# Evicting attention scores and v from PSUM: one strided read over four banks, contiguous writes, two engines

## The chip, the cores and the metric

The kernel runs on one core of a Trainium2 chip. The metric is the device time of one execution in microseconds (us), lower is better. Every kernel is therefore compared by its ratio to the kernel before in the same call.

Engine names: PE is TensorE (matmuls), PEld its weight loads, DVE is VectorE, ACT is ScalarE, POOL is GpSimd, SP the queue that issues the DMAs. PEclk is the share of TensorE's clock that was granted. PSUM is the memory that matmuls write to; this kernel uses it as 8 banks of 512 fp32 in each of 128 partitions. To evict is to copy a result from PSUM to SBUF, the engines' working memory; the profile calls these copies CAST. "L280" is line 280 of the kernel that is being shown. Lines differ by a few between kernels; the text says which is which.

## The reference, cut to what matters

```python
def _A_ref(x, wqkv, wo):            # S = 2048, D = 1024, 32 heads of 32
    q, k, v = ...                   # (x @ wqkv), split in heads
    idx = pos[:, None] - off[None, :]          # 8 keys per position, every second one
    logits = einsum('bhsd,bhswd->bhsw', q, k[idx]) * scale
    o = einsum('bhsw,bhswd->bhsd', softmax(masked logits), v[idx])
    return o @ wo
def _B_ref(x, w_in, w_sp, b_sp, w_out):        # gated MLP
    z = gelu(x @ w_in); z1, z2 = z[..., :Fh], layernorm(z[..., Fh:])
    return (z1 * (w_sp @ z2 + b_sp)) @ w_out
g = sigmoid((x * gate_w).sum(-1)); return g * A + (1 - g) * B
```

## The kernel before

The order of the work is: z2 (first quarter), attention in 8 groups of 4 heads, the rest of z2, z1, then the spatial and output stages. The change touches attention.

TensorE computes scores of 128 queries against a band of 135 keys. A *band set* is one to three such tiles for the 4 heads of a group. Head `h` goes to bank `4 + h`. ScalarE casts them to f16 in a staging tile where the 4 heads lie side by side, and a DMA writes them to DRAM, from where they come back sheared (shifted by one key from query to query) so that VectorE can work on 8 keys a query.

```python
def v_tile(hf, j):
    ps = low_bank()                                # banks 0 to 3
    ...  # 8 matmuls, 512 columns                                            (L250)
    nc.scalar.copy(_sub_ap(st, (j % 4) * 512, [[C, 4], [1, HG], [HG, DH]]),  # (L253)
                   ps[:].rearrange("p (g h d) -> p g h d", g=4, h=HG))
    ...  # DMA to v_d after every fourth tile

def band_set(g, x):                                # x = 0 .. 5
    ...
    for m in range(n):                             # n = 2, 3, 3, 3, 3, 2
        for h in range(HG):                        # HG = 4, KW = 135
            nc.tensor.matmul(banks[4 + h][:, m * KW + lo:(m + 1) * KW], ...)   # (L275)
    for h in range(HG):
        src = banks[4 + h][:, 0:n * KW].rearrange("p (m k) -> p m k", m=n)[:, :, lo:KW]
        nc.scalar.copy(st[:, 0:n, lo:KW, h], src)                             # (L280)
    ...  # DMA to band_d

for g in range(NG):                                # 8 groups
    main = ...   # q/k tiles of the next group (L243, cast in L245); v tiles in groups 0 and 3
    for x in range(6):
        band_set(g, x)
        ...      # a sixth of main after each set
    attend(g)    # VectorE: softmax, attn * v (L315 to L319); ScalarE: exp (L300)
...
for f in range(NF):                                # z1: 14 blocks
    for c in range(4):
        ...                                        # 8 matmuls (L425)
        nc.scalar.activation(z1s[:, c, :], ps[:], ACT.Gelu_apprx_tanh)       # (L427)
    sync.dma_start(z1_d[...], z1s)                 # z1s: one of two slots
...
load_raw(1)   # 8 transposing DMAs of half of w_sp (L183); the scheduler moves them up
```

An element of the band cast goes to `st[..., h]`, 4 f16 elements from the last: an 8-byte stride. The v cast also writes with an 8-byte stride.

## Time and profile before

Median 784.95 us (784.42 to 785.49, 2 runs).

| stretch (us) | what | what limits it |
|---|---|---|
| 66 to 327 | attention | ScalarE busy 228 of 261 us |
| 327 to 380.6 | rest of z2 | TensorE |
| 380.6 to 478.6 | z1 | TensorE |
| 478.6 to 786 | spatial, output | TensorE |

The table of stretches of the kernel before. Columns: busy us and number of instructions of PE, PEld, DVE, ACT, POOL, then granted TensorE clock, DMA share, GB/s.

```profile
core 0: us, PE busy (x) PEld busy (x) DVE busy (x) ACT busy (x) POOL busy (x), PEclk, DMA share, GB/s
66.00:327.00 261.00, 209.86 (x1235) 96.08 (x1235) 136.66 (x131) 228.21 (x307) 0.00 (x0) 0.90 0.52 145
```

The list by line, shapes kept apart, of the kernel before: count, then busy us and mean ns of one, then idle time before it. L280 is one of the four band casts, L253 the v cast, L245 the q/k cast, L493 a VectorE instruction that reads 512 fp32 from PSUM.

```profile
L280 ACT CAST arena<-bank_73 128x405 f16<-128x405 f32 x32 | 37.9, 1186 | 0.0
L253 ACT CAST arena<-bank_69 128x512 bf16<-128x512 f32 x8 | 11.6, 1450 | 0.0
L245 ACT CAST arena<-bank_67 128x512 bf16<-128x512 f32 x16 | 9.6, 598 | 13.2 <-PE bank_67 L243 13.2
L493 DVE TENSOR_TENSOR arena<-bank_69,arena 128x512 f16<-128x512 f32 x7 | 4.8, 686 | 0.7 <-PE bank_69 L435 0.6
```

The q/k cast reads with an 8-byte stride and writes contiguously: 598 ns for 512 elements. The v cast reads contiguously and writes with a stride: 1450 ns for as many. The band cast takes 1186 ns for 405.

The timeline of ScalarE in the kernel before (start, duration):

```profile
273.67 1.17 ACT L280 CAST arena<-bank_72 128x405 f16<-128x405 f32 x1
274.57 1.17 ACT L280 CAST arena<-bank_73 128x405 f16<-128x405 f32 x1
275.47 1.17 ACT L280 CAST arena<-bank_74 128x405 f16<-128x405 f32 x1
```

Neighbours overlap, so the rate is in the starts: 0.90 us apart, 2.2 ns an element.

The list of waits of the kernel before, 66 to 327 us (us in total, times, longest):

```profile
PE bank_74 L275 <- ACT arena L280: 13.5, 23, 0.7
PE bank_73 L275 <- ACT arena L280: 11.5, 21, 0.7
PE bank_71 L275 <- ACT arena L280: 10.3, 4, 4.9
PE bank_72 L275 <- ACT arena L280: 4.5, 10, 0.7
```

TensorE waits 39.8 us for ScalarE to free the band banks.

The chain of waits around the start of z1 (start, us, what), kernel before:

```profile
391.00 1.74 PE bank_69 L425 x8
392.74 0.07 SPq L183
...
405.06 3.57 DMA z_d<-arena
...
408.74 0.61 ACT arena L427
...
409.39 1.89 PE bank_71 L425 x8
```

```profile
406.37 1.89 PE L425 MATMUL bank_70<-arena 128*128 128x512 bf16 x8
409.39 1.89 PE L425 MATMUL bank_71<-arena 128*128 128x512 bf16 x8 [1.12 <-ACT arena L427]
```

The chain runs through transposes (L183) at 392.7 to 405, then a z1 write, then the cast that needed the slot.

### The profile page before, as it was taken

To read this page: it belongs to the slowest core of one execution; us is meant where nothing else is said; L and a number is where in the kernel's file an instruction comes from. 1 tells how busy PE (TensorE), PEld (TensorE's weight loads), DVE (VectorE), ACT (ScalarE), POOL (GpSimd) and SP (SyncE) were. 2 spreads that over 40 slices of the span, in tenths; PEclk is the share of its full clock that TensorE was granted. 3 is DMA by queue.
4 is the path that set the end of the run, shared out by engine and by line. 5 is a ranking of instruction groups with operands and counts; after the bars stand their busy time and mean duration, and the time that the engine had idled before them with its cause. 6 is when DMAs were issued, how large, how long until landed. Compare 5 with 4: busy or idle time off the path is not lost.

```text
span 785.7 us, 9516 instructions
## 1 busy us (share of the span) xinstructions
PE 720.4 (92%) x3672; PEld 335.9 (43%) x3672; DVE 361.6 (46%) x462; ACT 402.9 (51%) x649; POOL 6.0 (1%) x13
## 2 busy tenths in 40 slices
PE   5997868799778887899999999999999999999998
PEld 3554423355333333455444444444444444444443
DVE  1000027487192756795120008667888478332310
ACT  3456968999699889998523332212211121222221
POOL 0000000000000000001000000000000000000000
PEclk9999887999989779999999999999999999999999
DMA  8998563565426335605996242433646459983111
GB/s 213 243 98 127 157 178 117 157 179 139 120 85 195 106 125 164 197 2 142 214 220 179 76 133 81 108 77 84 213 109 168 121 114 205 183 163 95 52 41 40
DMA packets 238716, 106.45 MB, mean 135 GB/s; under 512 B 182864, under 2 KB 232016, under 8 KB 238672
## 3 DMA queue, kind: packets, MB, share of 16 engines
q1 hardware_dynamic: 237632, 105.86, 54.2%
q8 instruction: 28, 0.46, 0.3%
q10 hardware_dynamic: 1040, 0.00, 0.1%
q14 instruction: 16, 0.13, 0.0%
HBM read 45.10 MB, written 45.00 MB: 115 GB/s over the span
## 4 chain that ended last, share of the span: by engine, by line
PE 55%; SPq 2%; ACT 1%; DMA 1%; DVE 0%; issue 0%; ACTq 0%; DVEq 0%
PE bank_72 L435 6%; PE bank_71 L435 5%; PE bank_67 L435 5%; PE bank_68 L435 5%; PE bank_74 L435 5%; PE bank_70 L435 5%; PE bank_73 L435 3%; PE bank_69 L435 3%; SPq L183 2%; PE bank_71 L425 1%; PE bank_69 L425 1%; PE bank_67 L425 1%; PE bank_72 L425 1%; PE bank_68 L425 1%; PE bank_73 L425 1%; PE bank_74 L425 1%
## 5 line engine op out<-in xcount | busy, mean ns | idle before, releaser
L435 PEld LDWEIGHTS <-arena 128*128 128x128 f16 (+1 forms) x1400 | 137.0, 98 | 166.5 <-issue 1.6
L243 PEld LDWEIGHTS <-arena 128*128 128x128 bf16 x512 | 50.9, 104 | 67.7 <-issue 20.2
L210 PEld LDWEIGHTS <-arena 128*128 128x128 bf16 x512 | 50.3, 99 | 49.8 <-issue 5.0
L315 DVE TENSOR_TENSOR arena<-arena,att_A 128x8192 f16<-128x8192 bf16 x16 | 70.7, 4421 | 0.2
L425 PEld LDWEIGHTS <-arena 128*128 128x128 bf16 x448 | 43.8, 98 | 54.1 <-issue 1.4
L280 ACT CAST arena<-bank_73 128x405 f16<-128x405 f32 (+2 forms) x48 | 51.9, 1081 | 0.0
L280 ACT CAST arena<-bank_74 128x405 f16<-128x405 f32 (+2 forms) x48 | 51.8, 1079 | 0.0
L280 ACT CAST arena<-bank_72 128x405 f16<-128x405 f32 (+2 forms) x48 | 51.7, 1076 | 0.0
L250 PEld LDWEIGHTS <-arena 128*128 128x128 bf16 x256 | 36.6, 145 | 28.0 <-issue 10.5
L280 ACT CAST arena<-bank_71 128x405 f16<-128x405 f32 (+2 forms) x48 | 47.7, 993 | 0.3
L435 PE MATMUL bank_72<-arena 128*128 128x512 f16 x200 | 46.8, 379 | 1.0 <-ACT bank_72 L443 1.0
L435 PE MATMUL bank_70<-arena 128*128 128x512 f16 x200 | 46.9, 379 | 0.0
L435 PE MATMUL bank_71<-arena 128*128 128x512 bf16 x200 | 46.8, 379 | 0.0
L435 PE MATMUL bank_67<-arena 128*128 128x512 bf16 x200 | 46.8, 379 | 0.0
L435 PE MATMUL bank_68<-arena 128*128 128x512 f16 x200 | 46.8, 379 | 0.0
L435 PE MATMUL bank_74<-arena 128*128 128x512 f16 x200 | 46.8, 379 | 0.0
L482 DVE TENSOR_TENSOR arena<-arena 128x2048 f16<-128x2048 bf16 x14 | 17.1, 1222 | 62.5 <-DMA arena<-z_d 62.2
L275 PEld LDWEIGHTS <-arena 32*128 32x128 bf16 x512 | 14.5, 93 | 70.5 <-issue 70.5
L296 DVE TENSOR_TENSOR att_m<-att_L_108 128x256 f16<-128x256 f16 x4 | 1.2, 292 | 92.9 <-DMA att_L_108<-band_d_75 73.0
L464 DVE TENSOR_TENSOR arena<-arena 128x1024 f16<-128x1024 f16 (+2 forms) x30 | 17.8, 601 | 46.9 <-PE bank_74 L435 19.8
L243 PE MATMUL bank_70<-arena 128*128 128x512 bf16 x128 | 39.1, 459 | 0.0
L317 DVE TENSOR_TENSOR arena<-arena 128x4096 f16<-128x4096 f16 x16 | 36.6, 2290 | 0.4
(173 smaller groups left out, 1032.1 us busy)
## 6 DMA issues: line engine op xcount, KB each, us to landing
arena<-v_d SPq DMA_DIRECT2D x8, 960.0 KB, 6.3
z_d<-arena SPq DMA_DIRECT2D x14, 512.0 KB, 4.0
arena<-z_d SPq DMA_DIRECT2D x28, 256.0 KB, 3.2
zg_d<-arena SPq DMA_DIRECT2D x56, 128.0 KB, 2.2
arena<-zg_d SPq DMA_DIRECT2D x32, 224.0 KB, 3.3
arena<-in_A_wqkv_dram SPq DMA_DIRECT2D x16, 256.0 KB, 4.0
v_d<-arena SPq DMA_DIRECT2D x32, 128.0 KB, 2.3
o_d<-arena SPq DMA_DIRECT2D x4, 1024.0 KB, 6.0
```

The costliest lines, as they stand in the source:

```text
L183: inst = _orig_dmat(*a, **k)
L210: nc.tensor.matmul(ps[:, 0:N], xT[:, kt, i * P:(i + 1) * P], w2[:, kt, w2_off[c]:w2_off[c] + N], start=(kt == 0), stop=(kt == KT - 1))
L243: nc.tensor.matmul(ps[:], w[:, t, kt, :], xT[:, kt, 512 * c:512 * (c + 1)], start=(kt == 0), stop=(kt == KT - 1))
L250: nc.tensor.matmul(ps[:], _sub_ap(xT_flat, kt * S + j, [[NJ, P]]), wv[:, kt, 512 * hf:512 * hf + 512], start=(kt == 0), stop=(kt == KT - 1))
L275: nc.tensor.matmul(banks[4 + h][:, m * KW + lo:(m + 1) * KW], qt[hp, e, P * b:P * (b + 1)], kt_[hp, e, P * b - (W - 1) + lo:P * (b + 1)], ...
L280: nc.scalar.copy(st[:, 0:n, lo:KW, h], src)
L315: tt(prod.rearrange("p (w j d h) -> p w j d h", w=W, j=8, d=DH, h=HG), in0, in1, ALU.mult)
L317: tt(p3[:, 0:4, :], p3[:, 0:4, :], p3[:, 4:8, :], ALU.add)
L425: nc.tensor.matmul(ps[:], w1[:, kt, (f % 4) * P:(f % 4 + 1) * P], xT[:, kt, 512 * c:512 * (c + 1)], start=(kt == 0), stop=(kt == KT - 1))
L435: nc.tensor.matmul(bank[:], lhsT, rhs, start=(start and m == 0), stop=(stop and m == n - 1), skip_group_check=True)
L464: nc.vector.tensor_tensor(s_out[0], a21, a22, ALU.add)
L482: nc.vector.tensor_tensor(zgt, z1t, om, ALU.mult)
```

## The change

The order of the reading is turned. One instruction takes a whole band set: it reads the same column of banks 4, 5, 6, 7 (a 2 KB stride), and so writes 4 heads side by side, contiguously. Two of the six sets of a group go to VectorE. The v cast also reads with a stride and writes contiguously. PSUM becomes one tile, so that one access can span banks.

```diff
-    banks = [psum.tile([P, 512], F32, name=f"bank{b}") for b in range(8)]
+    psum_all = psum.tile([P, 8 * 512], F32, name="psum_all")
+    banks = [psum_all[:, 512 * b:512 * (b + 1)] for b in range(8)]
@@ v_tile
-        nc.scalar.copy(_sub_ap(st, (j % 4) * 512, [[C, 4], [1, HG], [HG, DH]]), ps[:].rearrange("p (g h d) -> p g h d", g=4, h=HG))
+        nc.scalar.copy(st[:, j % 4, :].rearrange("p (g d h) -> p g d h", g=4, h=HG), ps[:].rearrange("p (g h d) -> p g d h", g=4, h=HG))
@@ band_set
-        for h in range(HG):
-            src = banks[4 + h][:, 0:n * KW].rearrange("p (m k) -> p m k", m=n)[:, :, lo:KW]
-            nc.scalar.copy(st[:, 0:n, lo:KW, h], src)
+        dst = st[:, 0:n, lo:KW, :]
+        src = _sub_ap(psum_all, 4 * 512 + lo, [[KW, n], [1, KW - lo], [512, HG]])
+        if x in (2, 4):
+            with tc.high_priority():
+                nc.vector.tensor_copy(dst, src)
+        else:
+            nc.scalar.copy(dst, src)
```

## The prediction

> **What bounds the kernel now.** From 66 to 327 us ScalarE is the wall: the stretch table has it busy 228 of 261 us, 0.88, VectorE 137. The chain of waits lies on ScalarE at 321 to 327, then on TensorE, except for 392.7 to 405, where it runs through 16 transpose DMAs (38.5 us on the DMA queue from 366.4) ahead of the z1 writes.
>
> In the list by line the band evictions (source line 280) take 157 us of ScalarE and the v evictions (line 253) 32. A 128x405 band cast reads 1.17 us and starts 0.90 us after the last, 2.2 ns an element; a 128x512 v cast 1.45 us, starts 1.17 us apart, 2.3 ns. Both write with an 8-byte stride. The q/k cast (line 245) reads PSUM at an 8-byte stride but writes contiguously: 0.58 us for 512. So the write costs, not the read; the Trainium skill, "ScalarE: Activation LUTs", What ACT_TABLE_LOAD costs, gives 186 ns + 0.833 ns an element, which the q/k cast meets (0.61) and these two do not.
>
> **Costs of the change.** A three-tile set becomes one instruction of 1620 elements. ScalarE: about 1.55 us (estimate: the 128x1792 Square takes 1.72), against 3.6. VectorE: a 512-element PSUM read takes 0.686 us here, so 1.84 us for 1620 (estimate; the skill's "VectorE: DVE Perf Modes", Why PSUM operands drop a tier, allows no faster mode for fp32 from PSUM). I expect no penalty for crossing banks; no run shows that. v casts fall to about 0.6. Per group its bands fall from about 20 us to 5.2, v in the two v groups from 19 to 10; VectorE gains 2 x 1.84 = 3.7 a group, 29 in all.
>
> **Critical path.** TensorE needs per group without v 8 x 1.73 us of q/k plus 6 x about 0.43 of bands: 16.3 us against 22 to 33 today. The two v groups need and take 44: no gain. TensorE alone needs about 191 of the 261 us: at most 70 saved. But VectorE becomes the next wall: attention takes it about 22 us a group, so 26 with the evictions: attention on VectorE, now 112 to 360, can't end before about 315 to 330. It matters because o_d, the transposes and the z1 writes queue behind it, and because a VectorE eviction can stand behind a 4.4 us multiply while TensorE waits for banks. So I expect 25 to 60 us saved, middle 41.
>
> **Prediction: 744 us, 8 in 10 between 722 and 765.** Faster by over 2%: 0.90; within 2%: 0.08; slower: 0.02.
>
> **What would show each step.** Right: 48 band evictions instead of 192, 1.4 to 1.7 us on ScalarE, 1.75 to 1.95 on VectorE; v casts 0.58 to 0.72; ScalarE's busy total down by about 120 us from 403, VectorE's up by about 29 from 362; groups without v near 18 to 24 us; TensorE's waits for ScalarE evictions (40 us) mostly gone, some waits for VectorE evictions new. Wrong: bank-crossing evictions above 2.2 us; transposes still ending near 400.
>
> **What would make it wrong.** (1) Reading another bank at each element costs as much as the strided write did: then only the VectorE share and v gain, about 10 to 20 us. (2) The evictions' fixed places in VectorE's queue stall TensorE several us a set. (3) The gain meets a longer stall before z1, transposes still waiting for VectorE's last attention group. (4) Upward: the stall before z1 shrinks too: 715 to 722.

## More of the kernel before

ScalarE is busy 0.87 of the attention stage. TensorE's clock is granted only to 0.90.

## The result, and the profile after

Median 746.82 us (746.07 to 747.57, 2 runs) against 784.95: 38 us less. The ratio is 0.9514, 95% interval 0.9465 to 0.9564. Ratios in this document are the mean time of one kernel's fast runs over the mean of the other's of the same rounds, so not quite the ratio of the medians.

In the changed kernel L276 is the band matmul, L285 the ScalarE band eviction, L283 the VectorE one, L254 the v cast, L246 the q/k cast, L430 and L432 the z1 matmul and its activation, L184 the transposes. The stretch from 66 us to the last band set, now at 272 us (the first band matmul is at 51 us in both kernels):

```profile
66.00:272.00 206.00, 181.13 (x1219) 86.53 (x1220) 149.43 (x140) 101.63 (x147) 0.00 (x0) 0.95 0.63 174
```

ScalarE is busy 102 of 206 us, VectorE 149; the granted clock rose from 0.90 to 0.95. The list by line:

```profile
L246 ACT CAST arena<-psum_all 128x512 bf16<-128x512 f32 x64 | 37.4, 586 | 55.3 <-PE psum_all L244 55.0
L283 DVE CAST arena<-psum_all 128x1620 f16<-128x1620 f32 x16 | 29.4, 1838 | 48.0 <-PE psum_all L276 48.0
L285 ACT CAST arena<-psum_all 128x1620 f16<-128x1620 f32 x16 | 24.2, 1513 | 4.8 <-PE psum_all L276 4.7
L254 ACT CAST arena<-psum_all 128x512 bf16<-128x512 f32 x32 | 18.3, 587 | 37.6 <-PE psum_all L251 25.9 <-DMA v_d<-arena 11.8
```

A set of 1620 elements takes 1513 ns on ScalarE and 1838 on VectorE. Crossing a bank at every element costs nothing that can be seen: the fixed part and rate that the Trainium skill, "ScalarE: Activation LUTs", What ACT_TABLE_LOAD costs, states for an ACTIVATE (186 ns and 0.833 ns an element) give an estimate of 1536 ns for 1620. The v cast fell from 1450 to 587 ns, the time of the q/k cast.

The waits of TensorE for evictions, 66 to 272 us:

```profile
PE psum_all L276 <- DVE arena L283: 13.3, 7, 5.4
PE psum_all L276 <- ACT arena L285: 6.2, 3, 3.3
PE psum_all L251 <- ACT arena L254: 5.4, 1, 5.4
```

The 39.8 us for ScalarE's band casts became 6.2; 13.3 us for VectorE's are new. These waits are 20 us less in all, and do not make up the gain alone. From the first band matmul to the first z1 matmul the table of stretches reads, kernel before and then changed:

```profile
51.30:380.50 329.20, 278.06 (x1602) 133.18 (x1602) 170.17 (x179) 288.26 (x419) 4.00 (x3) 0.92 0.53 136
51.30:328.50 277.20, 252.33 (x1602) 125.14 (x1602) 195.85 (x195) 155.94 (x259) 5.06 (x3) 0.96 0.61 155
```

The matmuls are the same 1602. TensorE's idle time fell from 51 to 25 us, and its busy time from 278 to 252: 26 us each. The busy part goes with the clock: the clock records of these stretches show half speed for 54 us before and for 20 after, which is worth at most 17 us (an estimate, half of the difference). The other 9 are not explained. Each of the nine drops to half speed in the kernel before follows 3.4 us in which TensorE was busy for only 0.2 to 2.0. So the many waits of 0.7 us listed above went together with a lower clock.

The start of z1, timeline of TensorE:

```profile
349.82 6.42 PE L430 MATMUL psum_all<-arena 128*128 128x512 bf16 x29
366.71 1.87 PE L430 MATMUL psum_all<-arena 128*128 128x512 bf16 x4 [10.46 <-ACT arena L432]
```

and the chain of waits there:

```profile
359.80 2.79 SPq L184
362.69 3.27 DMA z_d<-arena
...
366.06 0.61 ACT arena L432
...
366.71 3.57 PE psum_all L430 x8
```

TensorE now does stand still: 10.46 us where it was 1.12. It came to z1 52 us earlier, but the transposes in front of the first z1 writes ended only 42 us earlier (362.7 against 405.0), because they queue behind the write of o_d, and that behind VectorE's last attention group. That group ended at 316.6 us against 360.6. The timeline of the DMA queue, kernel before (first two lines) and changed:

```profile
360.65 0.59 SPq L178 DMA_DIRECT2D o_d<-arena  x1
366.44 38.53 SPq L183 DMA_TRANSPOSE arena<-in_B_w_sp_dram  x16
316.62 0.59 SPq L179 DMA_DIRECT2D o_d<-arena  x1
321.98 40.61 SPq L184 DMA_TRANSPOSE arena<-in_B_w_sp_dram  x16
```

The table of stretches after this stop:

```profile
366.70:370.00 3.30, 3.29 (x8) 1.13 (x8) 2.66 (x2) 3.30 (x7) 0.00 (x0) 0.50 0.36 116
370.00:375.00 5.00, 5.00 (x20) 2.01 (x19) 0.00 (x0) 1.46 (x4) 0.00 (x0) 0.78 0.98 239
375.00:380.00 5.00, 5.00 (x25) 2.29 (x24) 0.00 (x0) 1.61 (x3) 0.00 (x0) 1.00 0.65 223
```

The granted clock is 0.50 in the first 3.3 us and full from 372.2 on by the clock records: the stop costs TensorE about 3 us more, as the 320 matmuls after it take 71.9 us against 69.2 before. The Trainium skill, "TensorE: Matmul & The Clock Gate", Part 1, states half rate after an idle window of about 3.4 us, and full rate again after a busy one. This stop agrees in kind: half speed was granted from 358.5 us, 2.3 us after TensorE had stopped, until 5.5 us after it started again.

The ledger of the two profiled runs, and of the later experiments. The start of z1 is TensorE's first z1 matmul, "z1" the time from there to the first spatial matmul, "longest stop" TensorE's longest idle time in z1:

| kernel | start of z1 | z1 | longest stop | spatial and output | span |
|---|---|---|---|---|---|
| before | 380.5 | 98.0 | 1.1 | 307.3 | 785.7 |
| changed | 328.5 | 110.0 | 10.5 | 307.3 | 745.8 |
| e1_v_only | 362.9 | 98.6 | 1.7 | 307.3 | 768.8 |
| e2_bands_act | 321.6 | 103.3 | 3.9 | 307.3 | 732.3 |
| e3_share_old_casts | 367.4 | 102.6 | 4.4 | 310.2 | 780.2 |
| e4_bank_by_bank | 369.1 | 107.2 | 8.0 | 307.3 | 783.6 |
| after_again | 330.9 | 110.4 | 11.5 | 307.5 | 748.8 |
| e5_raw_late | 328.8 | 96.7 | 0.0 | 310.5 | 736.0 |
| e7_act_late | 321.7 | 96.7 | 0.0 | 308.8 | 727.2 |
| e8_act_late_gatt | 321.7 | 96.7 | 0.0 | 309.1 | 727.5 |
| e2_again | 325.0 | 105.1 | 6.1 | 307.4 | 737.5 |
| e9_act_vector_load | 327.2 | 111.8 | 12.6 | 307.5 | 746.5 |
| e6_dve4 | 326.3 | 108.8 | 9.5 | 309.3 | 744.3 |
| e10_no_priority | 330.7 | 109.4 | 10.0 | 308.8 | 748.9 |

So the change gained 52.0 us up to z1 and gave 12.0 back in z1; 40 us are left (39.9 in the spans; the medians differ by 38, as the profiled execution of the kernel before took 787.8 us, 3 more than its median).

### The profile page after: what moved, and what is told of

Its sections match the earlier page's. It is cut to its first block, busy times and chain, and to the rows that moved or that the text cites. A ratio compares the mean times of both kernels' runs of the same rounds, so it can differ in the third digit from the quotient of the medians.

```text
span 745.8 us, 9289 instructions
## 1 busy us (share of the span) xinstructions
PE 697.2 (93%) x3672; PEld 328.2 (44%) x3672; DVE 387.0 (52%) x478; ACT 270.9 (36%) x489; POOL 7.0 (1%) x13
## 4 chain that ended last, share of the span: by engine, by line
PE 77%; DMA 8%; DVE 8%; SPq 3%; ACT 2%; issue 1%; ACTq 0%; DVEq 0%
PE psum_all L440 40%; PE psum_all L430 12%; PE psum_all L211 12%; PE psum_all L244 7%; PE psum_all L251 5%; DVE arena L320 3%; SPq L184 2%; ACT arena L285 1%; DVE arena L283 1%; DVE arena L322 1%; DMA band_d_74<-arena 1%; DMA arena<-in_A_x_dram 1%; PE psum_all L276 1%; SPq L179 1%; DMA band_d_68<-arena 1%
## 5 line engine op out<-in xcount | busy, mean ns | idle before, releaser
L440 PE MATMUL psum_all<-arena 128*128 128x512 f16 (+1 forms) x1400 | 302.6, 379 | 1.1 <-ACT psum_all L448 1.1
L244 PE MATMUL psum_all<-arena 128*128 128x512 bf16 x512 | 120.3, 388 | 0.0
L430 PE MATMUL psum_all<-arena 128*128 128x512 bf16 x448 | 99.7, 386 | 10.5 <-ACT arena L432 10.5
L211 PE MATMUL psum_all<-arena 128*128 128x448 bf16 (+1 forms) x512 | 102.2, 362 | 0.0
L430 PEld LDWEIGHTS <-arena 128*128 128x128 bf16 x448 | 44.4, 99 | 65.5 <-issue 14.4
L251 PE MATMUL psum_all<-arena 128*128 128x512 bf16 x256 | 58.5, 387 | 5.4 <-ACT arena L254 5.4
L432 ACT ACTIVATE arena<-psum_all 128x512 bf16<-128x512 f32 x56 | 32.7, 601 | 75.6 <-PE psum_all L430 50.8
L246 ACT CAST arena<-psum_all 128x512 bf16<-128x512 f32 x64 | 37.4, 586 | 55.3 <-PE psum_all L244 55.0
L283 DVE CAST arena<-psum_all 128x1620 f16<-128x1620 f32 x16 | 29.4, 1838 | 48.0 <-PE psum_all L276 48.0
L487 DVE TENSOR_TENSOR arena<-arena 128x2048 f16<-128x2048 bf16 x14 | 17.1, 1222 | 68.1 <-DMA arena<-z_d 68.0
L285 ACT CAST arena<-psum_all 128x1620 f16<-128x1620 f32 (+2 forms) x32 | 40.8, 1274 | 11.8 <-PE psum_all L276 11.5
L213 ACT ACTIVATE arena<-psum_all 128x448 bf16<-128x448 f32 x64 | 34.5, 542 | 25.1 <-PE psum_all L211 24.5
L448 ACT COPY psum_all<-psum_all 128x512 f32<-128x512 f32 x22 | 12.5, 570 | 84.7 <-PE psum_all L440 72.7
L276 PE MATMUL psum_all<-arena 32*128 32x135 bf16 (+1 forms) x512 | 17.1, 231 | 19.5 <-DVE arena L283 13.3
L254 ACT CAST arena<-psum_all 128x512 bf16<-128x512 f32 x32 | 18.3, 587 | 37.6 <-PE psum_all L251 25.9
```

The source lines that it names most:

```text
L211: nc.tensor.matmul(ps[:, 0:N], xT[:, kt, i * P:(i + 1) * P], w2[:, kt, w2_off[c]:w2_off[c] + N], start=(kt == 0), stop=(kt == KT - 1))
L213: nc.scalar.activation(z2[:, i, ZC * c:ZC * (c + 1)], ps[:, 0:ZC], ACT.Gelu_apprx_tanh, accum_out=s1[:, 4 * i + c:4 * i + c + 1])
L244: nc.tensor.matmul(ps[:], w[:, t, kt, :], xT[:, kt, 512 * c:512 * (c + 1)], start=(kt == 0), stop=(kt == KT - 1))
L246: nc.scalar.copy(dst[:, :, 256 * c:256 * (c + 1)], ps[:].rearrange("p (n e) -> p e n", e=2))
L251: nc.tensor.matmul(ps[:], _sub_ap(xT_flat, kt * S + j, [[NJ, P]]), wv[:, kt, 512 * hf:512 * hf + 512], start=(kt == 0), stop=(kt == KT - 1))
L283: nc.vector.tensor_copy(dst, src)
```

## The experiments

Three questions were open. Is it the form of the access (contiguous writes) or the sharing between engines that pays? Does VectorE's share help at all? And were the 12 us in z1 really given back to the DMA queue?

All kernels gave correct results. The first call had four kernels, 4 timed runs each; the others four each with 6.

### e1_v_only: the v cast alone

The changed kernel with the band evictions put back to the four casts of before. PSUM is one tile, v is written contiguously.

> Bands as before (four casts a set, all on ScalarE), PSUM as one tile, v casts written contiguously. Theory A (TensorE already bounds the two v groups, so v is not where the time came from): v casts 0.58 to 0.62 us instead of 1.45, 9 us of ScalarE freed in each v group, but total 778 to 785 us, at most 7 us faster than before. Rival (ScalarE bounds the v groups as well): 10 to 20 us faster, 765 to 775. A total equal to before also says that making PSUM one tile changes nothing by itself.

Measured: 774.91 us against 785.27 in the same rounds, ratio 0.9857 (0.9792 to 0.9922). The v cast took 621 ns. The gain of 10 us is at the lower edge of what the rival said; its interval, 6 to 16 us, still holds the 7 that my theory allowed, so the total does not decide. By the times of the last band write of each group (DMA timeline), group 0 was done at 94.1 us against 101.3, and the second v group took 40.7 us against 43.2. TensorE's wait for the v cast in group 0 fell from 8.1 to 3.1 us. But that v cast had itself been waiting for a DMA, the write that frees its staging slot (timeline of ScalarE, kernel before):

```profile
80.26 1.29 ACT L253 CAST arena<-bank_68 128x512 bf16<-128x512 f32 x1 [8.17 <-DMA v_d<-arena]
```

In e1 the cast waits 5.8 us for this write, in the changed kernel 11.8. So the v groups were not as purely bound by TensorE as I had reckoned, but the DMA queue held group 0 as well as the casts did. By the medians about a quarter of the whole gain belongs to e1. The profiled runs of the two kernels, which come from different calls, cannot place it better: their last band writes are 17.5 us apart, 9.7 of it in the two v groups and 7.8 in the others, where only PSUM as one tile is new. e1 does not separate the v cast from that tile.

### e2_bands_act: no share for VectorE

```diff
-        if x in (2, 4):
+        if x in ():
```

> The changed kernel with all six band sets of a group on ScalarE, one read each; VectorE takes none. Theory A (after the change VectorE is the next wall and its evictions cost more than they save): ScalarE's busy sum rises by about 25 us from 271 and stays far from full, VectorE's falls by 29 to about 358, attention on VectorE ends before 305 instead of 317, total 725 to 740 us. Rival (the sharing is needed, ScalarE would be the wall again): total 752 us or more.

Measured: 734.05 us, ratio 0.9331 (0.9278 to 0.9383), and 0.9306 when it was repeated (below). The changed kernel has 0.9514 and 0.9495. The sharing is not needed; without it the kernel is about 2% faster. ScalarE's busy sum is 291.9 us of a span of 732, VectorE's 360.8, and attention on VectorE ends at 303 us instead of 317. All of this was expected. In the ledger 6.9 us come before z1 and 6.7 in it. The list of waits, 66 to 272 us, shows for the band banks:

```profile
PE psum_all L276 <- ACT arena L285: 12.5, 6, 3.8
```

against 13.3 + 6.2 = 19.5 in the changed kernel.

### e3_share_old_casts: sharing without the new form

```diff
+        for h in range(HG):
+            src = banks[4 + h][:, 0:n * KW].rearrange("p (m k) -> p m k", m=n)[:, :, lo:KW]
+            if x in (2, 4):
+                with tc.high_priority():
+                    nc.vector.tensor_copy(st[:, 0:n, lo:KW, h], src)
+            else:
+                nc.scalar.copy(st[:, 0:n, lo:KW, h], src)
```

> Sharing alone: four casts a set with their 8-byte-stride writes as before, sets 2 and 4 on VectorE; v contiguous. Theory A (the contiguous write is the main part): ScalarE casts of 405 still start 0.9 us apart, total 758 to 775 us. Rival (taking load off ScalarE is what counts, in whatever form): within 5 us of the changed kernel's 747. Whether VectorE pays for the strided write is open: 0.57 us for 405 elements if not, about 1 us if it does.

Measured: 779.96 us, ratio 0.9919 (0.9863 to 0.9975). That is nearer to nothing than I expected, and no better than e1, which does not share (0.9857). VectorE's cast of 405 elements took 1094 ns, so VectorE pays for the stride too (list by line of e3_share_old_casts):

```profile
L283 DVE CAST arena<-psum_all 128x405 f16<-128x405 f32 x64 | 60.4, 1094 | 58.5 <-PE psum_all L276 56.8 <-ACT arena L246 1.7
```

ScalarE was relieved (busy 167 us of the stretch 66 to 327, against 228 in e1), yet the time did not follow. ScalarE's load alone was not what held attention.

### e4_bank_by_bank: one instruction, but strided writes

```diff
-        dst = st[:, 0:n, lo:KW, :]
-        src = _sub_ap(psum_all, 4 * 512 + lo, [[KW, n], [1, KW - lo], [512, HG]])
+        dst = st[:, 0:n, lo:KW, :].rearrange("p m k h -> p h m k")
+        src = _sub_ap(psum_all, 4 * 512 + lo, [[512, HG], [KW, n], [1, KW - lo]])
```

> The changed kernel with the order of elements in the eviction turned: still one instruction a set on the same engines, but bank by bank, so that reads are contiguous and writes go out at an 8-byte stride. Same result. Theory A (the strided write is the cost): 1620 elements take 3.5 to 3.8 us on ScalarE, total 755 to 775 us. Rival (four instructions were the cost, not the stride): 1.5 to 1.6 us, total 745 to 750. VectorE: 1.84 us if it does not mind the stride.

Measured: 787.32 us, ratio 1.0014 (0.9947 to 1.0082): the same time as before, although v and the sharing are those of the changed kernel. The list by line of e4_bank_by_bank:

```profile
L285 ACT CAST arena<-psum_all 128x1620 f16<-128x1620 f32 x16 | 60.9, 3805 | 4.0 <-PE psum_all L276 3.7
L283 DVE CAST arena<-psum_all 128x1620 f16<-128x1620 f32 x16 | 60.4, 3775 | 56.1 <-PE psum_all L276 55.2 <-ACT arena L246 0.9
L276 PE MATMUL psum_all<-arena 32*128 32x135 bf16 x448 | 14.7, 230 | 48.5 <-ACT arena L285 37.6 <-DVE arena L283 9.5 <-DVE att_m L303 1.2
```

The same elements in another order take 3805 instead of 1513 ns on ScalarE and 3775 instead of 1838 on VectorE. The number of instructions is not the cost; the stride of the writes is, and on both engines alike (2.3 ns an element). The size of the instruction was as expected, the total worse than expected.

The last line tells why, together with e3: the matmuls of a set wait 47.1 us for the evictions of the set before, although ScalarE is busy only 166 and VectorE 194 of the 261 us from 66 to 327. The four band banks are one buffer. The next set can start only when they are free, so the time from the last matmul of a set to the release of its banks counts, not the sum of the work on either engine. In e3 a bank comes free after each of four casts; in e4 all four come free at the end, 3.8 us later, and e4 is 7 us slower than e3. By this reading a second engine cannot help a loop in which one set is evicted at a time. The traces support it. Taken set by set from the timelines, the time from the end of a set's last matmul to the end of its eviction has a median of 3.8 us in the kernel before, in e1 and in e3, of 3.9 in e4, and of 1.7 in the changed kernel and in e2. I did not test it by giving the bands more banks, since eight banks leave no room for that.

### after_again and e5_raw_late: the wait at the start of z1

The transposes of the second half of w_sp are needed much later. In e5 each is ordered in the queue behind one z1 write:

```diff
+            t = sync.dma_start_transpose(raw_slots[c][:, :, a, :], wsp_v[row])
+            if c == 1:
+                tc.add_manual_dep(t.ins, z1_out[2 + a].ins.name, NOSYNC, ...)
```

> The changed kernel once more, for the comparison on one chip: 744 to 749 us.

> The changed kernel with the eight transposes of the second half of w_sp moved in the DMA queue from ahead of the first z1 write to behind the third to tenth z1 write, one each. Theory A (10 us of the gain are given back at the start of z1, where TensorE waits for z1 slots that wait for z1 writes that stand behind 16 transposes): the wait of TensorE at the start of z1 (10.5 us) falls under 2 us, total 9 to 12 us under the changed kernel. Rival (the wait is off the path, the spatial stage is bound elsewhere): total unchanged within 3 us.

Measured in the same rounds: the changed kernel 749.80 us (0.9495, 0.9464 to 0.9526; 0.8 us above what was expected), e5 737.69 us (0.9351, 0.9323 to 0.9380), 12 us less. The chain of waits of e5_raw_late over the start of z1 has no DMA left in it:

```profile
324.98 3.97 PE psum_all L211 x21
328.95 43.17 PE psum_all L433 x200
```

z1 takes 96.7 us instead of 110.4. The spatial and output stages take 3.0 us longer (310.5 against 307.5): TensorE's one stop there, at 592 us, is 2.5 us instead of 1.2, and the clock is then at half speed for 3.4 us; why the stop grew was not looked into. The loss in z1 was on the path, and its cause was the order of the DMA queue.

### e7_act_late and e8_act_late_gatt: both together

e7 is e2 with the change of e5. e8 also moves two small loads at the head of the DMA queue behind the first v writes.

> All bands on ScalarE in one read each (as e2_bands_act, 734 us) with the transposes moved as in e5_raw_late. In e2_bands_act TensorE waits only 3.9 us at the start of z1, so theory A expects only 3 to 6 us more: 728 to 731 us, less than e5 gains. Rival (both gain in full, independently): 722 to 725.

> e7_act_late, and the two small loads of g_att, which wait 11 us for the write of g_d at the head of the DMA queue in front of the first band and v writes, moved behind the first three v writes. The v casts of group 0 wait 9.8 us for v writes and TensorE 4.8 us for the casts in e2_bands_act. Expected: that wait of TensorE under 1 us, total 3 to 6 us below e7_act_late. If the four weight loads that follow fill the queue anyway, nothing.

Measured: e7 730.17 us (0.9257, 0.9229 to 0.9284), e8 728.84 us (0.9234, 0.9203 to 0.9266), in the same rounds as e5. e7 gains 7.5 us on e5; against e2 it is 0.9257 to 0.9331. The two improvements overlap, as expected: without the VectorE share the transposes come earlier, so there is less stop to remove. What is left of the difference lies before z1, which begins at 321.7 us in e7 and at 328.8 in e5. e8 differs from e7 by 1.3 us, inside the noise, and its stated purpose failed: TensorE's wait for the v casts went from 6.2 to 4.0 us, not under 1. Both beat the changed kernel by 2.5 to 2.7%.

### e2_again and e9_act_vector_load: what the share on VectorE costs

e9 gives VectorE work of the same size and, by the scheduler, about the same places as its evictions, but no engine waits for it. (Six of the 48 adds ran at 39 to 42 us, before the first VectorE eviction of the changed kernel at 66.)

```diff
+        if x in (2, 4):
+            with tc.high_priority():
+                for r in range(3):
+                    load = nc.vector.tensor_tensor(spare[:], spare[:], spare[:], ALU.add)
+                    tc.add_manual_dep(load.ins, evict.ins.name, NOSYNC, ...)
```

> e2_bands_act once more, for the comparison on one chip: 730 to 737 us.

> e2_bands_act (all bands on ScalarE) with VectorE given as much work as its evictions cost it, 3 adds of 0.61 us on a spare tile per set 2 and 4 (29 us in all), which no other engine waits for. Tells apart what made the shared version 13 us slower. Theory L (VectorE's load: its last attention group, the o_d write and the transposes behind it end later): attention on VectorE ends near 317 us, total 743 to 749. Theory P (TensorE waiting for VectorE evictions that stand behind long multiplies, 13 us in the changed kernel): total as e2_again within 3 us.

Measured: e2_again 741.56 us (0.9306, 0.9268 to 0.9344), e9 747.25 us (0.9376, 0.9339 to 0.9412). The absolute numbers are higher than expected because this call was slow (before: 797.25); e2_again missed its range by 5 us, and e9 lies in that of theory L only for this reason. The added load was 29.2 us (48 adds of 608 ns). It cost 5.7 us, less than half of the 13 that the share costs, so neither theory is right alone. In the profiled runs attention on VectorE ended 7.6 us later (315.1 against 307.5), z1 began 2.2 us later, and z1 took 6.7 us longer. That is about the z1 part of the loss of the changed kernel against e2 (6.7 us; 5.3 from after_again to e2_again), reproduced by load alone. The part before z1 (6.9 us) is mostly not, and the 2.2 us are less than the 3.4 by which the two profiles of e2 differ. There the evictions themselves, which TensorE waits for, remain as the likely cause; no run tests them without the load.

### e6_dve4 and e10_no_priority

e6 has `x in (1, 2, 3, 4)` for VectorE, e10 drops the raised priority.

> The changed kernel with sets 1 to 4 of each group on VectorE instead of 2 and 4, so that VectorE has twice the evictions (59 us instead of 29). From none to two sets the end of attention on VectorE went from 303 to 317 us and the total from 734 to 747. Theory A: it goes on like this, attention ends at 330 to 345 us, TensorE's waits for VectorE evictions double to 25 us or more, total 758 to 775. Rival (what mattered was only the first step): 745 to 752.

> The changed kernel without the raised priority of VectorE's evictions, so that their places in VectorE's queue are by program order and readiness. If a VectorE eviction standing behind attention's multiplies is what costs TensorE, this makes it worse: waits of TensorE for VectorE evictions over 20 us (13 with priority), total 750 to 765. If the place makes no difference, 745 to 750.

Measured: e6 747.26 us (0.9371, 0.9335 to 0.9406), e10 750.46 us (0.9418, 0.9382 to 0.9454). In both the first theory missed. e6 lies in the range of its rival and e10 0.5 us above that of its second branch, though this call was a slow one. With twice the changed kernel's evictions on VectorE its attention did end later than with none, at 325.2 us against 307.5 in e2_again, but z1 began only 1.3 us later, the total was only 5.7 us over e2_again, and by the ratios e6 is faster than the changed kernel (0.9371 against 0.9495). TensorE waited 17.3 us for VectorE evictions, not 25 or more. The DMA queue of e6 shows one reason:

```profile
330.60 28.16 SPq L184 DMA_TRANSPOSE arena<-in_B_w_sp_dram  x10
358.86 1.20 SPq L179 DMA_DIRECT2D z_d<-arena  x2
360.11 10.15 SPq L184 DMA_TRANSPOSE arena<-in_B_w_sp_dram  x3
```

Here the scheduler put two z1 writes after the tenth transpose and not after the sixteenth, so z1's stop (9.5 us) did not grow with VectorE's end. Without priority (e10) the waits for VectorE evictions were 12.0 us, no more than with it. So "the more on VectorE, the later" is not a rule: the static order of the queues, which changes with every edit, counts too. What stays is that all three shared versions are slower than none shared.

## Why the prediction was right, point by point

- *ScalarE is the wall in attention.* Right in effect. Its casts held TensorE's banks for 39.8 us of waits, which fell to 6.2. The prediction did not have the clock: half of the 52 us before z1 is TensorE's own busy time, which fell by 26 us at a higher granted clock. e3 corrects the reason: relieving ScalarE without shortening the eviction of a set gained less than 1%. It is the time of one set's eviction that counted, more than the engine's load.
- *The write costs, not the read; no penalty for crossing banks.* Right: 1513 and 1838 ns were measured for 1.55 and 1.84 us estimated. e4 shows it with only the order of elements changed.
- *v groups "need and take 44: no gain".* Off: e1 gained 10 us in all (6 to 16 by its interval). Group 0 ended 7.2 us earlier; there TensorE had an 8.1 us wait for a v cast, itself held by a v write, that the average over the group hid.
- *Groups without v near 18 to 24 us.* By the last band writes of groups 1, 2, 4, 5 and 6 they were 34.4, 26.2, 32.2, 25.3 and 27.5 us and became 26.7, 16.3, 26.2, 20.1 and 17.1. The mean, 21.3, is right; only one of the five lies in the range.
- *ScalarE down by about 120 us, VectorE up by about 29.* Measured from 403 to 271 (132) and from 362 to 387 (25).
- *VectorE's attention ends at 315 to 330, and o_d, transposes and z1 writes queue behind it.* Right: it ended at 316.6, and the transposes at 362.7. I named a longer stop before z1 as a risk; it came, 10.5 us, and e5 gets 12 us back by moving eight transposes.
- *The sum.* 41 us were expected, 38 came. That it is so near is in part luck: 41 was the middle of a range, and the prediction had no figure for either part, the 52 us gained before z1 and the 12 given back in z1.
- *What the prediction did not say:* that VectorE's share was a loss. I treated the shared work as given and reckoned its cost, without asking for the total without it. ScalarE would have had room: 102 of 206 us busy after the change.

## What to carry to other kernels

When an eviction needs a transposed order, put the stride on the PSUM read and keep the SBUF write contiguous: at 2-byte elements the 8-byte write stride cost 2.5 times on ScalarE and 2.1 times on VectorE, while the read stride, even from bank to bank, cost nothing. Shorten the eviction before sharing it: where one buffer of banks is emptied at a time, as here, a second engine did not shorten the loop, and its added load delayed what it did next. Where many short waits disappear, read the granted clock too: here TensorE's busy time fell as much as its idle time. After a large gain look at the next stage's queue, since DMAs ordered for the old timing (here eight transposes needed much later) can take part of it back.

## What the Trainium skill lacked or had wrong

- "SBUF — State Buffer", Door 1: The DMA port swizzle, in its note on cachelines, says that two or more consecutive accesses in a 16-byte line run at full bandwidth (and that each crossing to a new line has a penalty, of no stated size). f16 writes at an 8-byte stride put two in each line, and took 3805 ns for 1620 elements on ScalarE and 3775 on VectorE, against 1513 and 1838 contiguous. The measurement decides.
- "PSUM — Partial Sum Buffer", Specifications, says of non-contiguous access only that it slows matmuls. No page that I read gives the cost for an engine that reads PSUM with a stride: here none, at 8 bytes (598 ns for 512 elements), 128 bytes (587 ns) and 2 KB with a change of bank at every element (1513 ns for 1620).
- "VectorE: DVE Perf Modes" has no row for the effect of a strided output on a copy from PSUM; here it doubled the time, to the same 2.3 ns an element as on ScalarE. "Vector Engine (DVE) Microarchitecture Reference", The SBUF access granule: adjacent pairs, does time strided writes on VectorE, but of 4-byte words in SBUF, not of 2-byte results copied from PSUM.
